# Reordering the first two batches of a fused sliding-window attention and hard-swish MLP: row-wise values in batch 0, weights asked for ahead of batch 2's second half

## The chip, the cores and the metric

The kernel runs on one core of a Trainium2 chip. The metric is the device time of one execution in microseconds (us). The core has five engines with an instruction queue each: TensorE (PE, with its weight loads shown as PEld), VectorE (DVE), ScalarE (ACT), GpSimd (POOL) and SyncE (SP). Each runs its own instructions in the order of the program and waits for the others by semaphores. DMAs are asked for by SP, ACT and POOL.

## The reference

Eight batches of eight heads with 576 positions of 64 channels go through causal attention in a window of 128 positions with a linear bias per head. The result is laid out as 4608 tokens of 512 channels and goes through an MLP with a hard-swish between its two matrices.

```python
rel = pos[:, None] - pos[None, :]
scores = where((rel >= 0) & (rel < 128), q @ k.T / 8 - slope[h] * abs(rel), -1e9)
attn = softmax(scores) @ v                     # 8 x 8 x 576 x 64
x = attn.transpose(0, 2, 1, 3).reshape(4608, 512)
h = x @ w_in                                   # 512 x 2048
out = (h * clip(h + 3, 0, 6) / 6) @ w_out      # 2048 x 512
```

## The kernel before

**Attention.** A group g is a pair of heads of one batch (`NP`, four, of them to a batch): batch b has the groups 4b to 4b+3, so batch 0 is groups 0 to 3, batch 1 groups 4 to 7, and group 8 opens batch 2. Since the window is 128, a block of 128 queries needs the scores with its own block of keys (the diagonal, `scores_diag`) and with the block ahead of it (the off-diagonal, `scores_off`). The bias comes either out of a table that a matmul adds into PSUM (`tables_diag`, `tables_off`, used for the diagonals of batch 0 and the off-diagonals of batches 0 and 1) or out of the exponential's bias on ACT, with a mask laid by POOL afterwards (`exp_diag`, `affine_select`). `attend` multiplies all five query blocks of a group with v and divides by the row sums on DVE; `back` transposes the result into `xT`, the MLP's input.

**Queries and keys.** For batch 0 each pair of heads is loaded by itself (`load_run`), cast to bf16 (`prepare`) and transposed by PE (`transposes`, 18 transposes of 64 by 64 for q and as many for k); each transpose bank is copied into `qTb` or `kTb`. Batches 1, 2 and part of 3 go by "doubles" of four heads: `load_double` (two requests of 288 KB), `prepare_double` (two casts on POOL), and `wide_double` or `double` (nine transposes, then one or two copies). `dp` is the half of the batch: dp 0 serves its first two groups, dp 1 its last two.

**MLP.** Tokens go in nine blocks of 512. For a block, 16 steps `moe_up` of four matmuls make the hidden layer (ACT takes a relu, DVE a scalar_tensor_tensor into `gbuf`), and 16 steps `moe_down` multiply with `w_out`. `fill(n)` issues the next n steps of that list, if the attention of their tokens is done (`done`). `up_begin` issues three of a step's four matmuls early. The order of everything else is written by hand: the scheduler keeps the program's order on each engine.

**Order at the start.** `first_batch` runs scores and exponentials of the four groups, then four times `attend` and `back`; two `up_begin` and the first fills stand between the last `back` and the double transposes of batch 1. `second_batch` runs groups 4 to 7 with fills between them, then `attend` and `back` of the four. `segment` does the rest, one group at a time: in the round of g it issues the scores and exponentials of g, the values of g - 1, and `stage_next(g)`, which holds the casts for what follows.

**Rooms and queues.** `ldbuf` 0 to 3 take the loads: q and k in 0 and 1, v of batches 0, 1 and 2 in 2, 3 and 2. Until w_out arrives, `w_out_sb` holds the probabilities of batch 0, and `gbuf[1]` those of batch 1. SP asks for q, v and k and for the stores; POOL asks for `w_in` (four chunks) and `w_out` (four chunks), in line with its casts and masks. The chunk of w_in numbered i is needed from step 4i of the first block on. A `memset` of one element into a room holds a later request back until that memset has run. PSUM banks: two of two banks each for scores ("sc"), one "av", two "h", one "o".

Of the kernel before, what the change touches and what calls it, by code (L numbers as in the profile page):

```python
# [10 lines left out]
FP32 = mybir.dt.float32  # L11
# [7 lines left out]
def kernel(  # L19
# [18 lines left out]
    LAST = S - 4 * 128  # L38
    SP = NQ * 128
    W = D + 1  # L40
    RP, RT = 64, 9
    slopes = [2.0 ** (-8.0 * (h + 1) / H) for h in range(H)]
    n_ms = d_ff // 128
    n_ks = d_model // 128
# [39 lines left out]
    ld = {}  # L84
    src_of = {"q": q, "k": k, "v": v}

    runs = {nm: ldbuf[i][:, 0:NP * RT * D].rearrange("p (g c) -> p g c", g=NP)
            for i, nm in enumerate("qk")}

    def load_run(g, nm, eng):  # L90
        b, hp = divmod(g, NP)
        eng.dma_start(out=runs[nm][:, hp, :],
                      in_=src_of[nm][b, 2 * hp:2 * hp + 2, :, :].rearrange(
                          "e (p t) d -> (e p) (t d)", t=RT))

    def load_double(b, dp, nm, eng):
        for e in range(2):
# [102 lines left out]
                                    in_=tbuf.rearrange("p h j c -> p (h j c)"))  # L200

    st = {}

    def prepare(g, copies):
        for nm, copy in zip("qk", copies):
            pr = prs.tile([128, RT * D], BF16, tag=f"pr{nm}", name="pr",
                          padded_shape=[128, 2 * RT * D])
            copy(out=pr, in_=runs[nm][:, g % NP, :])
            st[g, nm] = pr

    def transposes(g, copies):
        b, hp = divmod(g, NP)
        for nm, dst, copy in (("q", qTb[b % 2], copies[0]), ("k", kTb[b % 2], copies[1])):
            src = st.pop((g, nm))
            tp = ps_h.tile([128, RT, RP], BF16, tag="h", name="tp", padded_shape=[128, 16, 64])
            for t in range(RT):
                for e in range(2):
                    r = slice(e * D, (e + 1) * D)
                    nc.tensor.transpose(tp[r, t, :], src[r, ts(t, D)], ident[r, r])  # L219
            copy(out=dst[:, hp, :, :].rearrange("p j c -> p (j c)")[:, 0:S].rearrange(  # L220
                "p (a t) -> p a t", t=RT), in_=tp.rearrange("p t a -> p a t"))

    def prepare_double(b, dp, copies, nms="kq", early=None):
        for nm, copy in zip(nms, copies):
# [113 lines left out]
    def exp_full(g):  # L338
        for e in range(2):
            exp_diag(g, e)  # L340
        exp_off_full(g)
# [76 lines left out]
    def by_xbar(g):  # L418
        return g >= XB and g != XB + 2 and g != XB + 3
# [120 lines left out]
    def stage_next(g):  # L540
        b, hp = divmod(g, NP)
        nb = b + 1
        if g == 2 * NP:
            cast_tokens(2, "v")
        for n in LOADS.get(g, "").split():
            load_tokens(int(n[1]), n[0])
        if nb == 3 and hp < 2:
            prepare_double(3, hp, (P,), "k")
        if nb == 3 and hp == 1:
            cast_tokens(3, "q")  # L550
            xbar(3, "q")
        elif nb < B and nb > 3 and hp < 2:
            cast_tokens(nb, "qk"[hp])
            xbar(nb, "qk"[hp])
        if VCAST.get(g):
            cast_tokens(VCAST[g], "v")

    def first_batch():
# [6 lines left out]
        scores_diag(0)  # L565
        prepare(1, (P, V))
        transposes(1, (V, V))
        scores_off(0)
        exp_full(0)
        scores_diag(1)  # L570
        prepare(2, (P, P))
        tables_off(1)
        transposes(2, (V, V))
        scores_off(1)
        exp_full(1)
        scores_diag(2)
        prepare(3, (P, V))
        tables_off(2)
        transposes(3, (V, V))
        scores_off(2)  # L580
        exp_full(2)
        scores_diag(3)
        scores_off(3)
        exp_full(3)
        cast_v(0, 0, V)
# [12 lines left out]
        attend(2)  # L598
        back(1)
        prepare_double(1, 0, (P, P), early=second_w_in)  # L600
        attend(3)
        back(2)
        up_begin(0, 0, 3)
        back(3)
        wide_double(1, 0, "q", V)
        prepare_double(1, 1, (P, P))
        load_w_in(2)
        load_w_in(3)
        for dp in range(2):
            for nm in "kq":  # L610
                load_double(2, dp, nm, nc.sync)
        up_begin(0, 1, 3)
        done[0] = NP
        fill(1)
        wide_double(1, 0, "k", A)
        fill(2)

    def second_batch():
        for g in range(NP, 2 * NP - 1):
            if g < NP + 2:  # L620
                wide_double(1, 1, "kq"[g - NP], V)
            scores_diag(g)
            exp_diag(g, 0)
            exp_diag(g, 1)
            fill(1 if g == NP + 2 else 2)
            scores_off(g)
            exp_off_full(g)
            fill(2 if g == NP + 2 else 1)
            if g == NP + 1:
                cast_tokens(1, "v")  # L630
        for i in range(4):
            load_w_out(i)
        g = 2 * NP - 1
# [24 lines left out]
        wide_double(2, 0, "q", A)  # L658
        up_begin(1, 0, 3)
        back(2 * NP - 1)  # L660
        up_begin(1, 1, 3)
        done[0] = 2 * NP
        fill(2)
        scores_diag(2 * NP)
        scores_off(2 * NP)

    FILLS = {g: (1, 1, 1, 2, 0, 1, 1) for g in (9, 10, 11, 13, 14, 15)}

    def segment(lo, hi, fills):
        for g in range(lo, hi + 1):  # L670
            f = fills(g)
            if by_xbar(g - 2):
                done[0] = g - 1
            if lo < g < hi and g != 3 * NP + 1:
                scores(g)
            turn = {2 * NP: (2, 1, "k"), 2 * NP + 1: (2, 1, "q"),
                    2 * NP + 2: (3, 0, "k"), 2 * NP + 3: (3, 1, "k")}.get(g)
# [12 lines left out]
            if g > lo:  # L690
                values(g - 1, (0, 1, 2))
            fill(f[2])
            if g < hi:
                exp_off(g, 0)
            fill(f[3])
            if g < hi:
                exp_off(g, 1)
            if g > lo:
                values(g - 1, (3, 4))
            fill(f[4])  # L700
            if g > lo and by_xbar(g - 1):
# [14 lines left out]
    with tc.manual_schedule(engines=every):  # L716
        load_run(0, "k", nc.scalar)
        load_run(0, "q", nc.sync)
        load_run(1, "k", nc.scalar)
        load_run(1, "q", nc.sync)  # L720
        for g in (2, 3):
            load_run(g, "k", nc.scalar)
            load_run(g, "q", nc.sync)
        load_tokens(0, "v")
        constants()
        memsets()
        memsets_later()
# [36 lines left out]
```

## Time and profile before

| | |
|---|---|
| Median of three runs | 323.27 us (323.09 to 324.08) |
| The profiled execution | 323.3 us, its span 321.6 us, 1.7 us around it |
| PE busy | 312.4 us, 97% of the span |
| PEld, DVE, ACT, POOL busy | 167.6, 173.0, 195.6, 141.1 us |
| DMA | 51.90 MB moved, mean 161 GB/s |
| Granted clock of TensorE | 0.998 |

The span is that of the instructions in the trace. Busy time is the union of an engine's instructions; DMA requests and semaphores do not count. A matmul's shown duration has a tail that overlaps the next one: 512 columns are shown as some 0.38 us each while eight in a row take 1.73 us, 0.216 us from start to start.

### The profile page before, as it was taken

Reading aid. Unit: us, or ns where it says so; the run is one execution under the profiler, and the core shown is the slowest. Engines: PE = TensorE matmul, PEld = TensorE weight load, DVE = VectorE, ACT = ScalarE, POOL = GpSimd, SP = SyncE. Lnnn points to the kernel's source line nnn. Section 1 sums busy time; section 2 is a strip of 40 time slices with the busy share of each in tenths; the row PEclk is TensorE's granted clock in tenths of the full one; section 3 lists DMA queues with packets and bytes.
Section 4 is the critical chain, followed back from the end, with each engine's and each line's share of the span. In section 5 each row is a group of like instructions: output and inputs, shape, how many; then the busy total and the mean of one; then the engine's idle time right before and its main releaser. Section 6 shows DMA issues by size and latency. Waiting matters only on the chain.

```text
span 321.6 us, 7050 instructions
## 1 busy us (share of the span) xinstructions
PE 312.4 (97%) x2738; PEld 167.6 (52%) x2738; DVE 173.0 (54%) x338; ACT 195.6 (61%) x334; POOL 141.1 (44%) x249
## 2 busy tenths in 40 slices
PE   7889999999999999999999999999999999999996
PEld 5565465455555554554667654554554444444443
DVE  6667674554456555555555555555655455455510
ACT  3758976877767766766676667666764344244401
POOL 8455493594493767366745665463331000000000
PEclk9999999999999999999999999999999999999999
DMA  7999999899999999999999989922112200000112
GB/s 276 202 333 208 247 270 196 210 258 194 212 248 166 244 201 203 193 229 199 192 199 202 237 173 212 214 72 86 23 53 66 75 34 35 33 33 33 67 53 77
DMA packets 131425, 51.90 MB, mean 161 GB/s; under 512 B 118976, under 2 KB 123328, under 8 KB 131392
## 3 DMA queue, kind: packets, MB, share of 16 engines
q1 hardware_dynamic: 126160, 45.36, 66.2%
q0 software_dynamic: 4224, 4.19, 8.2%
q10 hardware_dynamic: 1008, 1.90, 1.6%
q8 instruction: 21, 0.34, 0.5%
q14 instruction: 12, 0.10, 0.1%
HBM read 36.70 MB, written 9.44 MB: 143 GB/s over the span
## 4 chain that ended last, share of the span: by engine, by line
PE 82%; DMA 10%; SPq 2%; POOL 2%; DVE 1%; ACT 1%; issue 1%; POOLq 0%
PE ops L501 37%; PE hps L451 33%; DMA w_out_sb<-in_moe_w_out_dram 5%; DMA ldbuf<-in_v_dram 3%; PE scd L296 3%; DMA ldbuf<-in_k_dram 2%; PE av L391 2%; SPq L112 2%; PE av L383 2%; PE sco L328 1%; PE ops L482 1%; PE w L153 1%; POOL w_out_sb L171 1%; PE tp L219 0%; ACT kTb L244 0%
## 5 line engine op out<-in xcount | busy, mean ns | idle before, releaser
L471 DVE SCALAR_TENSOR_TENSOR gbuf<-r,hps 128x512 bf16<-128x512 f32 x144 | 98.7, 687 | 102.5 <-ACT r L470 100.2
L470 ACT ACTIVATE r<-hps,bias 128x512 f32<-128x512 f32 x144 | 98.9, 689 | 88.9 <-PE hps L451 88.7
L451 PE MATMUL hps<-xT,w_in_sb 128*128 128x512 bf16 (+1 forms) x640 | 144.8, 358 | 0.5 <-ACT xT L438 0.3
L501 PE MATMUL ops<-w_out_sb,gbuf 128*128 128x512 bf16 x560 | 137.8, 379 | 0.3 <-DMA w_out_sb<-in_moe_w_out_dram 0.3
L451 PEld LDWEIGHTS <-w_in_sb 128*128 128x128 bf16 x640 | 59.2, 98 | 54.8 <-issue 0.8
L501 PEld LDWEIGHTS <-gbuf 128*128 128x128 bf16 x560 | 51.8, 98 | 56.7 <-issue 0.6
L354 POOL TENSOR_SCALAR_AFFINE_SELECT pd<-pd 128x512 bf16<-128x512 bf16 x48 | 29.7, 634 | 34.5 <-ACT pd L351 34.5
L364 POOL TENSOR_SCALAR_AFFINE_SELECT po<-po 128x512 bf16<-128x512 bf16 x48 | 30.3, 636 | 32.5 <-ACT po L361 32.3
L351 ACT ACTIVATE pd<-scd,bias_d 128x512 bf16<-128x512 f32 x48 | 31.7, 685 | 4.7 <-PE scd L296 4.7
L510 DVE COPY osb<-ops 128x512 f32<-128x512 f32 x33 | 22.7, 687 | 20.4 <-PE ops L501 20.2
L361 ACT ACTIVATE po<-sco,bias_o 128x512 bf16<-128x512 f32 x48 | 33.0, 688 | 0.0
L194 POOL CAST tbuf<-ldbuf 128x512 bf16<-128x512 f32 (+1 forms) x45 | 25.6, 614 | 16.7 <-DMA qTb<-tbuf 9.0
L402 DVE TENSOR_TENSOR avs<-av,rc 128x384 bf16<-128x384 f32 (+1 forms) x48 | 23.6, 491 | 1.6
L391 PEld LDWEIGHTS <-pd 128*128 128x128 bf16 x192 | 14.3, 97 | 8.3 <-issue 0.5
L383 PE MATMUL av<-vbuf,po 128*128 128x65 bf16 x192 | 18.0, 193 | 0.0
L391 PE MATMUL av<-vbuf,pd 128*128 128x65 bf16 x192 | 17.3, 194 | 0.3 <-ACT kTb L244 0.3
L187 POOL CAST vbuf<-ldbuf 128x1024 bf16<-128x1024 f32 x14 | 14.3, 1044 | 4.3 <-DMA ldbuf<-in_v_dram 4.3
L383 PEld LDWEIGHTS <-po 128*128 128x128 bf16 x192 | 14.3, 98 | 2.9 <-DVE avs L402 0.5
L367 ACT ACTIVATE p4buf<-sco,bias_d 128x64 bf16<-128x64 f32 x48 | 15.5, 324 | 0.0
L227 POOL CAST pr<-ldbuf 128x576 bf16<-128x576 f32 x20 | 12.9, 670 | 5.0 <-DMA ldbuf<-in_k_dram 3.1
L296 PE MATMUL scd<-qTb,kTb 64*128 64x128 bf16 x256 | 12.7, 219 | 1.7 <-DVE kTb L220 0.9
L296 PEld LDWEIGHTS <-kTb 64*128 64x128 bf16 x256 | 7.2, 94 | 13.4 <-issue 9.7
(96 smaller groups left out, 217.4 us busy)
## 6 DMA issues: line engine op xcount, KB each, us to landing
out_dram<-osb SPq DMA_DIRECT2D x33, 256.0 KB, 2.4
ldbuf<-in_v_dram SPq DMA_DIRECT2D x32, 256.0 KB, 5.6
ldbuf<-in_q_dram SPq DMA_DIRECT2D x20, 256.0 KB, 4.9
ldbuf<-in_k_dram SPq DMA_DIRECT2D x16, 256.0 KB, 4.5
ldbuf<-in_q_dram SPq DMA_DIRECT2D x12, 288.0 KB, 7.3
ldbuf<-in_k_dram SPq DMA_DIRECT2D x12, 288.0 KB, 7.6
w_in_sb<-in_moe_w_in_dram POOLq DMA_DIRECT2D x4, 512.0 KB, 8.8
w_out_sb<-in_moe_w_out_dram POOLq DMA_DIRECT2D x4, 512.0 KB, 11.6
```

The lines of the kernel that those rows point to most:

```text
L194: nc.gpsimd.tensor_copy(out=tbuf[:m, :, j, :], in_=s[:m, j, :, :].rearrange("p (i e) d -> p i (e d)", e=2))
L296: nc.tensor.matmul(scd[:, e, ts(j, 128)], lhsT=kT[r, j, :], rhs=qT[r, j, :], start=first, stop=first or j == 3)
L351: nc.scalar.activation(out=pd[:, e, :, :].rearrange("p j c -> p (j c)"), in_=sc[:, e, :], func=ACT.Exp, bias=bias_d[:, h:h + 1], scale=scale)
L354: nc.gpsimd.affine_select(out=pd[:, e, :, :], in_=pd[:, e, :, :], pattern=[[0, 4], [1, 128]], channel_multiplier=-1, base=0, compare_op=AL ...
L361: nc.scalar.activation(out=po[:, e, :, :].rearrange("p j c -> p (j c)"), in_=sc[:, e, :], func=ACT.Exp, bias=bias_o[:, h:h + 1], scale=scale)
L364: nc.gpsimd.affine_select(out=po[:, e, :, :], in_=po[:, e, :, :], pattern=[[0, 4], [-1, 128]], channel_multiplier=1, base=-1, compare_op=A ...
L383: nc.tensor.matmul(out_av, lhsT=po[:, e, qt % 4, :], rhs=vb[:, qt - 1, h, :], start=True, stop=False)
L391: nc.tensor.matmul(out_av, lhsT=d, rhs=vb[:, qt, h, :], start=(qt == 0), stop=True)
L451: nc.tensor.matmul(hps[:, lo:hi], lhsT=w_in_sb[:, ks, ts(ms, 128)], rhs=xT[:, ks, ds(src, hi - lo)], start=(ks == 0), stop=(ks == n_ks - 1))
L470: nc.scalar.activation(out=r6, in_=hps, func=ACT.Relu, bias=bias3[:, 0:1], scale=1.0 / 6.0)
L471: nc.vector.scalar_tensor_tensor(out=gts[nt][:, ms, :], in0=r6, scalar=1.0, in1=hps, op0=ALU.min, op1=ALU.mult)
L501: nc.tensor.matmul(ops[nt, sub], lhsT=gts[nt][:, ms, ts(sub, 128)], rhs=w_out_sb[:, ms, :], start=(ms == 0), stop=(ms == n_ms - 1))
```

## The change

In batch 0, a run of q or k is laid out as 96 partitions with six positions of both heads each, so that one transpose serves both heads: 6 for q and 6 for k where there were 18 each. The last run lies in `ldbuf[3]`. The order of transposes, score matmuls and exponentials is another, `memsets_later` moves from ahead of the first batch to behind batch 1's first transposes, and the values are worked out by rows of queries over several groups: `values_first` (blocks 0 to 2 of one group), `values_row` (one block of several groups), `values_last` (blocks 0 to 3 of group 3). Block 4, the last 64 positions, is worked out after `scores_diag(4)`. The two `up_begin` of block 0 are gone: the first MLP step stands behind `scores_diag(5)`.

In batch 1, the order of doubles, scores and fills is another, and `load_w_out` stands directly behind the casts of v. Of batch 2, the second double (dp 1) and v are asked for at the end of `second_batch`, behind a one-element memset on DVE; the casts of that double move from `second_batch` to `stage_next(8)`, its key transposes from the round of group 8 to that of group 9, and its query transposes to later in that same round.

```diff
     def prepare(g, copies):
...
-            pr = prs.tile([128, RT * D], BF16, tag=f"pr{nm}", name="pr",
-                          padded_shape=[128, 2 * RT * D])
-            copy(out=pr, in_=runs[nm][:, g % NP, :])
+            pr = prs.tile([RN, RK, 2, D], BF16, tag=f"pr{nm}", name="pr",
+                          padded_shape=[128, RT, 2, D])
+            copy(out=pr.rearrange("p t e d -> p e t d"),
+                 in_=runs[nm, g % NP].rearrange("p e (t d) -> p e t d", t=RK))
...
     def stage_next(g):
         if g == 2 * NP:
+            prepare_double(2, 1, (P, P))
+            for dp in range(2):
+                load_double(3, dp, "k", nc.sync)
+            load_tokens(3, "q")
             cast_tokens(2, "v")
...
     def first_batch():
...
+        scores_diag(3)
+        values_first(0, "av")
+        scores_off(3)
+        exp_full(3)
+        values_first(1, "h")
         cast_v(0, 3, V)
         cast_v(0, 4, P)
+        values_first(2, "h")
...
-        attend(0)
-        attend(1)
-        back(0)
-        attend(2)
-        back(1)
+        values_row((0, 1, 2), 3, "av")
+        values_last(3)
+        back_first(0, "o", (A,))
+        back_first(1, "h", (A,))
+        back_first(2, "h", (A,))
         prepare_double(1, 0, (P, P), early=second_w_in)
-        attend(3)
-        back(2)
-        up_begin(0, 0, 3)
-        back(3)
-        wide_double(1, 0, "q", V)
+        back_first(3, "o", (A, V))
+        wide_double(1, 0, "k", V)
+        wide_double(1, 0, "q", A)
+        memsets_later()
+        scores_diag(NP)
+        exp_diag(NP, 0)
+        exp_diag(NP, 1)
+        values_row((0, 1), 4, "av")
+        values_row((2, 3), 4, "h")
         prepare_double(1, 1, (P, P))
-        load_w_in(2)
-        load_w_in(3)
-        for dp in range(2):
-            for nm in "kq":
-                load_double(2, dp, nm, nc.sync)
-        up_begin(0, 1, 3)
+        for nm in "kq":
+            load_double(2, 0, nm, nc.sync)
+        scores_off(NP)
+        exp_off_full(NP)
+        back_row("o", A)
         done[0] = NP
-        fill(1)
-        wide_double(1, 0, "k", A)
-        fill(2)

     def second_batch():
...
+        scores_diag(NP + 1)
+        exp_diag(NP + 1, 0)
+        exp_diag(NP + 1, 1)
         load_w_in(2)
         load_w_in(3)
+        fill(2)
+        scores_off(NP + 1)
+        exp_off_full(NP + 1)
         fill(1)
+        wide_double(1, 1, "k", V)
+        fill(1)
+        wide_double(1, 1, "q", V)
+        fill(3)
+        cast_tokens(1, "v")
         for i in range(4):
             load_w_out(i)
+        g = NP + 2
...
         prepare_double(2, 0, (P, P))
-        nc.gpsimd.memset(ldbuf[2][:, 0:1], 0.0)
-        load_tokens(2, "v")
-        prepare_double(2, 1, (P, P))
-        for dp in range(2):
-            load_double(3, dp, "k", nc.sync)
-        load_tokens(3, "q")
...
+        nc.vector.memset(ldbuf[1][:, ds(2 * RT * D, 1)], 0.0)
         fill(2)
         scores_diag(2 * NP)
         scores_off(2 * NP)
+        for nm in "kq":
+            load_double(2, 1, nm, nc.sync)
+        load_tokens(2, "v")
```

More of the change, by code (lines that the diff above doesn't have):

```diff
@@ L40 @@
     W = D + 1
-    RP, RT = 64, 9
+    RT = 9
     slopes = [2.0 ** (-8.0 * (h + 1) / H) for h in range(H)]
@@ L85 @@
     src_of = {"q": q, "k": k, "v": v}
-    runs = {nm: ldbuf[i][:, 0:NP * RT * D].rearrange("p (g c) -> p g c", g=NP)
-            for i, nm in enumerate("qk")}
+    RN, RK = 96, 6
+    runs = {}
+    for i, nm in enumerate("qk"):
+        for hp in range(NP):
+            room, at0 = (ldbuf[i], hp * 2 * RK * D) if hp < 3 else (ldbuf[3], i * 2 * RK * D)
+            runs[nm, hp] = room[0:RN, ds(at0, 2 * RK * D)].rearrange("p (e c) -> p e c", e=2)
     def load_run(g, nm, eng):
         b, hp = divmod(g, NP)
-        eng.dma_start(out=runs[nm][:, hp, :],
+        eng.dma_start(out=runs[nm, hp],
                       in_=src_of[nm][b, 2 * hp:2 * hp + 2, :, :].rearrange(
-                          "e (p t) d -> (e p) (t d)", t=RT))
+                          "e (a t) d -> a e (t d)", t=RK))
     def load_double(b, dp, nm, eng):
@@ L213, in transposes @@
         for nm, dst, copy in (("q", qTb[b % 2], copies[0]), ("k", kTb[b % 2], copies[1])):
[L214 to L219, printed above, removed]
+            src = st.pop((g, nm)).rearrange("p t e d -> p t (e d)")
+            tp = ps_h.tile([128, RK, RN], BF16, tag="h", name="tp", padded_shape=[128, 8, 128])
+            for t in range(RK):
+                nc.tensor.transpose(tp[:, t, :], src[:, t, :], ident[0:RN, 0:RN])
             copy(out=dst[:, hp, :, :].rearrange("p j c -> p (j c)")[:, 0:S].rearrange(
-                "p (a t) -> p a t", t=RT), in_=tp.rearrange("p t a -> p a t"))
+                "p (a t) -> p a t", t=RK), in_=tp.rearrange("p t a -> p a t"))
     def prepare_double(b, dp, copies, nms="kq", early=None):
@@ L556, in stage_next, with values_first, normed @@
             cast_tokens(VCAST[g], "v")
+    def values_first(g, tag):
+        av = BANKS[tag].tile([128, 3, 2, W], FP32, tag=tag, name="av",
+                             padded_shape=[128, 3, 2, 85])
+        av_matmuls(g, range(3), lambda qt, e: av[:, qt, e, :])
+        normed(av, avs0[:, g, 0:3, :, :], 3)
+    def normed(av, to, n):
+        rc = small.tile([128, 4, 2, 1], FP32, tag="rcn", name="rcn")
+        nc.vector.reciprocal(rc[:, 0:n], av[:, :, :, D:W])
+        nc.vector.tensor_tensor(out=to, in0=av[:, :, :, 0:D],
+                                in1=rc[:, 0:n].to_broadcast([128, n, 2, D]), op=ALU.mult)
@@ new lines, in values_row @@
+    def values_row(gs, qt, tag):
+        n = len(gs)
+        if tag == "sc":
+            wide = ps_sc.tile([128, 2, 512], FP32, tag="sc", name="wide")
+            av = wide.rearrange("p s (g c) -> p (s g) c", c=256)[:, :, 0:2 * W].rearrange(
+                "p g (e c) -> p g e c", e=2)[:, 0:n]
+        else:
+            av = BANKS[tag].tile([128, n, 2, W], FP32, tag=tag, name="av",
+                                 padded_shape=[128, 3, 2, 85])
+        for i, g in enumerate(gs):
+            av_matmuls(g, (qt,), lambda _, e: av[:, i, e, :])
+        normed(av, avs0[:, gs[0]:gs[0] + n, qt, :, :], n)
@@ new lines, in values_last, with back_first @@
+    def values_last(g):
+        wide = ps_sc.tile([128, 2, 512], FP32, tag="sc", name="wide")
+        av = wide.rearrange("p s (g c) -> p (s g) c", c=256)[:, :, 0:2 * W].rearrange(
+            "p g (e c) -> p g e c", e=2)
+        av_matmuls(g, range(4), lambda qt, e: av[:, qt, e, :])
+        normed(av, avs0[:, g, 0:4, :, :], 4)
+    def back_first(g, tag, copies):
+        tp = BANKS[tag].tile([128, 512], BF16, tag=tag, name="tb", padded_shape=[128, 1024])
+        for j in range(4):
+            nc.tensor.transpose(tp[:, ts(j, 128)],
+                                avs0[:, g, j, :, :].rearrange("p e d -> p (e d)"), ident)
+        n = 512 // len(copies)
+        for i, copy in enumerate(copies):
+            copy(out=xT[:, g, ds(i * n, n)], in_=tp[:, ds(i * n, n)])
@@ L558, in first_batch, with back_row @@
+    def back_row(tag, copy):
+        tp = BANKS[tag].tile([128, NP, 128], BF16, tag=tag, name="tb",
+                             padded_shape=[128, 8, 128])
+        for g in range(NP):
+            nc.tensor.transpose(tp[:, g, :], avs0[:, g, 4, :, :].rearrange("p e d -> p (e d)"),
+                                ident)
+        copy(out=xT[:, :, ds(512, LAST)], in_=tp[:, :, 0:LAST])
     def first_batch():
@@ L565, in first_batch @@
         scores_diag(0)
+        scores_off(0)
+        exp_full(0)
         prepare(1, (P, V))
         transposes(1, (V, V))
-        scores_off(0)
-        exp_full(0)
         scores_diag(1)
         prepare(2, (P, P))
-        tables_off(1)
         transposes(2, (V, V))
@@ L575, in first_batch @@
         exp_full(1)
+        prepare(3, (P, P))
         scores_diag(2)
-        prepare(3, (P, V))
-        tables_off(2)
         transposes(3, (V, V))
@@ L581, in first_batch @@
         exp_full(2)
[L582 to L585, printed above, removed]
+        cast_v(0, 0, P)
         cast_v(0, 1, P)
@@ L675, in segment @@
                 scores(g)
-            turn = {2 * NP: (2, 1, "k"), 2 * NP + 1: (2, 1, "q"),
+            turn = {2 * NP + 1: (2, 1, "k"),
                     2 * NP + 2: (3, 0, "k"), 2 * NP + 3: (3, 1, "k")}.get(g)
@@ L699, in segment @@
                 values(g - 1, (3, 4))
+            if g == 2 * NP + 1:
+                double(2, 1, "q", 0, "av", A)
             fill(f[4])
+            if g == 2 * NP + 1:
+                double(2, 1, "q", 1, "h", V)
             if g > lo and by_xbar(g - 1):
```

26 lines of the change are left out of this document (11 added, 15 removed).

## The prediction

> **What bounds the kernel now.** I read the page first, then busy time by stretch, then PE's and POOL's timelines up to 70 us. The first two lines are busy time and the chain that ended last.
>
> ```profile
> PE 312.4 (97%) x2738; PEld 167.6 (52%) x2738; DVE 173.0 (54%) x338; ACT 195.6 (61%) x334; POOL 141.1 (44%) x249
> ...
> PE 82%; DMA 10%; SPq 2%; POOL 2%; DVE 1%; ACT 1%; issue 1%; POOLq 0%
> ```
>
> PE is busy 97% of the span and carries 82% of the chain. The next view, columns PE, PEld, DVE, ACT, POOL, clock, DMA share, GB/s, shows where it is not full.
>
> ```profile
> 7.00:19.00 12.00, 9.78 (x248) 6.45 (x240) 7.98 (x14) 8.72 (x9) 5.54 (x10) 1.00 1.11 234
> 19.00:25.00 6.00, 5.09 (x81) 3.93 (x78) 4.38 (x9) 2.34 (x5) 3.78 (x6) 1.00 1.10 352
> 25.00:42.00 17.00, 17.00 (x178) 9.01 (x176) 11.06 (x15) 16.76 (x26) 9.71 (x15) 1.00 1.13 244
> 42.00:62.00 20.00, 19.05 (x192) 10.64 (x190) 12.37 (x22) 14.73 (x26) 12.13 (x20) 1.00 1.09 205
> ```
>
> From 25 to 42 us PE never rests, with ACT close behind (16.76 of 17 us). After 42 us only about 1 us is missing up to 62. The holes lie ahead of 25 us, where scores, exponentials and copies of batch 0 alternate and busy time counts the tails of short matmuls. So the time is PE's work plus PE's waits. The change leaves that work as it is: 144 small transposes, 36 of which take 0.76 us, become 48 wider ones, which I put at 0.05 us (nine of 128 by 128 take 0.67 us with their tail), 0.6 us per group in either form. It is a question of waits alone. PE's timeline behind batch 0:
>
> ```profile
> 22.00 0.59 PE L451 MATMUL hps<-xT,w_in_sb 128*128 128x512 bf16 x2
> 22.89 0.38 PE L451 MATMUL hps<-xT,w_in_sb 128*128 128x512 bf16 x1 [0.29 <-ACT xT L438]
> ...
> 23.38 0.67 PE L254 MATMUL tp<-ident,pr 128*128 128x128 bf16 x9
> 23.88 1.03 PE L451 MATMUL hps<-xT,w_in_sb 128*128 128x512 bf16 x4
> 24.75 0.67 PE L254 MATMUL tp<-ident,pr 128*128 128x128 bf16 x9
> 25.25 1.24 PE L451 MATMUL hps<-xT,w_in_sb 128*128 128x512 bf16 x5
> 26.33 0.67 PE L254 MATMUL tp<-ident,pr 128*128 128x128 bf16 x9
> 26.93 0.40 PE L296 MATMUL scd<-qTb,kTb 64*128 64x128 bf16 x8
> ...
> 59.05 1.02 PE L501 MATMUL ops<-w_out_sb,gbuf 128*128 128x512 bf16 x4 [0.33 <-DMA w_out_sb<-in_moe_w_out_dram]
> ```
>
> While batch 1's q and k arrive, PE is fed with 12 up matmuls (2, 1, 4 and 5) and the third double; `scores_diag(4)` follows at 26.93. POOL's timeline gives the arrivals and requests that matter:
>
> ```profile
> 20.93 2.17 POOL L227 CAST pr<-ldbuf 128x576 bf16<-128x576 f32 x3 [1.49 <-DMA ldbuf<-in_k_dram]
> ...
> 27.22 0.67 POOL L227 CAST pr<-ldbuf 128x576 bf16<-128x576 f32 x1 [0.73 <-DMA ldbuf<-in_q_dram]
> 27.83 1.48 POOL L166 DMA_DIRECT2D w_in_sb<-in_moe_w_in_dram  x2
> ...
> 47.86 2.49 POOL L227 CAST pr<-ldbuf 128x576 bf16<-128x576 f32 x4
> ...
> 60.68 0.29 POOL L370 TENSOR_SCALAR_AFFINE_SELECT p4buf<-p4buf 128x128 bf16<-128x128 bf16 x1
> ...
> 62.56 1.05 POOL L187 CAST vbuf<-ldbuf 128x1024 bf16<-128x1024 f32 x1 [0.60 <-DMA ldbuf<-in_v_dram]
> ```
>
> The row at 20.93 is three casts for dp 0, the last begun on q's arrival at about 22.4 and done at 23.1. The w_in request at 27.83 holds chunks 2 and 3. The four casts at 47.86 are those of batch 2's second double, in an empty stretch; 60.68 is group 8's last mask, and batch 2's v casts follow.
>
> **Part 1, batch 0: no gain on the path.** Runs of 288 KB in 96 partitions move the same bytes; a cast there is 768 elements per partition for 576, estimated 0.67 x 4/3 = 0.89 us on POOL. With no memsets ahead of it, POOL begins q of group 1 at its landing, 6.1 instead of 6.53. I lay the order out by row times (copy 0.76, exponential of 1024 columns 1.02, transposes 0.6): diagonal exponentials begin at 8.4, 11.1, 13.5 and 15.7 (before 8.38, 10.69, 13.56, 16.41), the last exponential ends at 17.9 (18.36). Values, divisions (0.2 + 0.56 us) and `back_first` end on PE at 21.2, where the last `back` ended at 23.5. This gain of 2.3 us hides behind an arrival: batch 1's q is cast at 23.1 as before, since SP asks for the same loads in the same order and the w_in chunk 0 request moves only from 12.4 to about 12.7.
>
> **Part 2, the front: +2.0 us.** PE has no MLP step to put there now. Double k at 21.9, double q at 23.1 to 23.6, its copy on ACT 1.11 us, `scores_diag(4)` at 25.0. Then two `values_row` (0.5), `scores_off(4)` (0.85 with tables), `back_row`, `scores_diag(5)`, and the first step at 27.3. By 27.25 the kernel before had done 12 up matmuls (12 x 0.216 = 2.6 us) and a third double (0.5); the changed one has `scores_off(4)` and `scores_diag(5)` ahead (0.85 + 0.24). It is 2.6 + 0.5 - 1.1 = 2.0 us of PE work behind. Bounds: 1.4, if ACT and DVE hand over without delay; 3.0, if the copies queue (the key copy sits behind `back_first(3)`'s DVE half, which waits for ACT's half).
>
> **Part 3, to the values of batch 1: +0.2 and +1.0.** Double copies of 1.35 us on DVE stand between the hidden-layer steps; laid out, step 6 waits for a bank, `scores_diag(6)` for the query copy, step 7 for a bank, 0.7 us in all, against some 0.5 us of small waits before. The w_in request for chunks 2 and 3 now stands on POOL behind 2.7 us of memsets, the masks of group 4 (waiting for exponentials that end at 26.6), four casts (2.5) and the masks of group 5: about 30.9 for 27.83. Queued behind it are the v casts and w_out. A chunk takes 6.3 to 9.5 us from request to landing (median 8.8), so it lands at 37.2 to 40.4; step 8 wants it at 37.2. The wait is 0 to 3.2 us; I take 1.0, nearest to chunk 2's own 6.3 us, as v of batch 1 was ahead of it there and here is nearly through. The Trainium skill ("DMA: Bandwidth & Descriptors", Queues, rings and completion order) has each DMA engine go round the queues packet by packet, so POOL's chunk would share with SP's loads rather than stand behind them; by it the wait would be nearer 0.5 us and the sum 0.5 us less. The trace agrees in kind: a v load asked for at 27.98 landed after 10.47 us, while the two chunks requested from 27.83 passed it.
>
> **Part 4, w_out and batch 2: -0.5 and +1.2.** w_out is asked for at about 35 for 41.2; its four chunks, 3.2 to 3.4 us between landings in the trace, follow w_in's last and are through by 57, so the 0.33 us wait at 59.05 goes, and a bank wait beside the moved double, 0.2. The doubles (2, 1) are asked for at about 53, when DVE reaches its memset (which waits for casts long done and delays no hidden-layer step behind it), and v behind them on SP; 1.2 + 1.2 MB arrive by 62 to 65 at the 200 GB/s of those slices. They are late for nothing by themselves. But their four casts (2.49 us) leave an empty stretch for the place between 60.68 and 60.92: group 8's last mask, then four casts, then v. Two v casts (2 x 1.0) end 4.5 us after the mask; before, values of group 8 began 3.6 us after it (64.53), of which 0.3 was the w_out wait. PE waits 1.2 us, part of it already in front of double (2, 1, k). Bounds 0.3 (casts end before PE comes) and 1.8. Masks of group 9 come 2.7 us later on POOL, 71.5 for 69; their values want them after 75. The other moved requests (k and q of batch 3) stand behind one store on SP, and their casts have over 2 us of room.
>
> **Sum.** Against the profiled 323.3 us (span 321.6 and 1.7 around it), which is the median to 0.03: 2.0 + 0.2 + 1.0 - 0.5 + 1.2 = +3.9, so 327.2 us. All lows: 1.4 + 0 + 0 - 0.7 + 0.3 = +1.0, 324.3; all highs: 3.0 + 0.5 + 3.2 - 0.3 + 1.8 = +8.2, 331.5; both together are unlikely, 324.3 to 329.5 is this case's own range.
>
> **Rivals.**
> *ACT was the bound (faster).* If ACT and not PE sets the stretch from 25 to 42 us, the change gives it group 4's exponentials at 25.3 instead of 27.68 and one copy of 1.11 us less, for 0.3 more: its 17.1 us of work up to group 7's last exponential would end at 25.3 + 16.3 = 41.6, for 42.1. With 0.5 of part 4 and the casts in time, 323.3 - 0.5 - 0.5 = 322.3, or 321.9 if batch 1's back chain gains too. For it: 16.76 of 17 us. Against: PE is 17.00 of 17 and has none of ACT's waits there. It decides if PE does its steps with ACT never idle over 0.3 us between 25 and 42. Chance 0.10.
> *Most of it is covered.* q and k of batch 1 land earlier (at best 0.9 us, then DVE's key copy holds `scores_diag(4)` at 24.05), w_in arrives in time, the casts cost 0.3: 2.0 - 0.9 + 0.2 - 0.5 + 0.3 = +1.1 or somewhat less, 324.0. For: the first requests go out unhindered. Against: the DMA share is over 1.0 there. Chance 0.12.
> *The clock falls.* In this trace the first matmuls ran at half pace (512 columns in 0.43 us until about 6.4 us, from 1.43), and later ones at 0.216. From 19.3 to 25.0 the changed PE has only 2.0 us of work, all transposes. If that returns it to half pace for as long as at the start, 5 us, 2.5 us of work takes twice its time: 327.2 + 2.5 = 329.7. Before, the stretch from 19 to 25 us (5.09 of 6 busy) showed no slow matmul. Chance 0.10. The Trainium skill ("TensorE: Matmul & The Clock Gate", Part 1) states that an idle window of about 3.4 us halves the clock and that as long a busy one restores it; by it the cost would be an estimated 1.7 us.
> *v of batch 2 comes late.* The change would not do what it says if w_out, asked for sooner, were not through by 57 and held the double and v behind it: v's fourth piece landing after 67 adds what is over, up to 2 us: 329. Chance 0.08.
>
> **How the numbers follow.** About 0.3%, 1 us, is what a measurement of this kernel can tell from no change. Forecast 0.60 (327.2), clock 0.10, late v 0.08, covered 0.12 (of it 0.05 slower by over 0.3%, 0.07 within), ACT 0.10 (of it 0.09 faster by over 0.3%, 0.01 within). Slower 0.83, same 0.08, faster 0.09. The range leaves out the ACT case below and the highest ends above: 323.4 to 330.0.
>
> **What would show it.** `scores_diag(4)` near 25 and the first up matmul near 27.3, PE's busy time in 19 to 25 us under 4 us; the w_in request near 31 and a wait for w_in before step 8; no wait for w_out; the casts of the double (2, 1) on POOL just behind group 8's masks and PE waiting for POOL near 66 to 68; the rest of the chain shifted as a whole. I am wrong if the first up matmul stands before 25 us, or if PE's waits behind 27 us add up to less than before.

## The result and the profile after

The changed kernel takes 333.4 us (median of 4 runs, 332.55 to 334.4) where the kernel before takes 323.4 beside it. The ratio is 1.031, with a 95% interval of 1.027 to 1.034. It is slower, as forecast, but by 10.0 us and not by 3.9, and lies above the range. The profiled execution took 333.56 us, with a span of 331.8. Executions over 1.5% longer than the fastest of the same kernel count as disturbed and are left out of the ratios, as 342.03 us of the kernel with w_in early, whose trace is therefore not read, and 335.79 us of the kernel with batch 2 as before.

The first view is the page: busy time, and the granted clock in 40 slices (one slice is 8.3 us).

```profile
PE 314.0 (95%) x2642; PEld 168.0 (51%) x2642; DVE 172.7 (52%) x343; ACT 196.0 (59%) x335; POOL 141.1 (43%) x250
...
PEclk9995999999999999999999999999999999999999
```

PE's busy time grew by only 1.6 us (314.0 for 312.4), and its share fell from 97 to 95%. The new thing is the 5 in the clock row: in the fourth slice, 25 to 33 us, TensorE ran at half pace. By stretch (columns as in the prediction: PE, PEld, DVE, ACT, POOL, clock, DMA share, GB/s):

```profile
19.00:25.00 6.00, 3.07 (x64) 2.52 (x60) 3.51 (x10) 2.58 (x5) 2.91 (x7) 0.99 1.09 345
25.00:32.00 7.00, 5.40 (x64) 3.74 (x62) 2.48 (x5) 3.29 (x4) 5.08 (x13) 0.52 1.19 263
32.00:42.00 10.00, 9.45 (x72) 4.79 (x72) 6.75 (x9) 7.52 (x14) 9.29 (x13) 1.00 0.96 216
42.00:62.00 20.00, 17.93 (x212) 10.54 (x213) 11.71 (x22) 14.85 (x23) 4.88 (x8) 1.00 0.86 150
```

From 19 to 25 us PE is busy for 3.07 of 6 us (before 5.09). Then 5.40 of 7 us are busy, but at 0.52 of the clock, at which the same work takes longer. PE's and POOL's timelines show what it waits for:

```profile
22.60 0.38 PE L602 MATMUL tb<-ident,gbuf 128*128 128x128 bf16 x4 [0.23 <-ACT xT L606]
24.50 0.81 PE L259 MATMUL tp<-ident,pr 128*128 128x128 bf16 x9 [1.51 <-POOL pr L232]
25.70 1.14 PE L259 MATMUL tp<-ident,pr 128*128 128x128 bf16 x9 [0.40 <-POOL pr L232]
28.05 0.61 PE L301 MATMUL scd<-qTb,kTb 64*128 64x128 bf16 x8 [1.21 <-ACT qTb L261]
...
31.93 1.90 PE L456 MATMUL hps<-xT,w_in_sb 128*128 128x512 bf16 x8
...
43.54 0.82 PE L456 MATMUL hps<-xT,w_in_sb 128*128 128x512 bf16 x3 [1.73 <-DMA w_in_sb<-in_moe_w_in_dram]
```

```profile
29.52 1.22 POOL L359 TENSOR_SCALAR_AFFINE_SELECT gbuf<-gbuf 128x512 bf16<-128x512 bf16 x2 [1.86 <-ACT gbuf L356]
30.70 2.48 POOL L232 CAST pr<-ldbuf 128x576 bf16<-128x576 f32 x4
33.14 1.21 POOL L359 TENSOR_SCALAR_AFFINE_SELECT gbuf<-gbuf 128x512 bf16<-128x512 bf16 x2
34.31 1.51 POOL L170 DMA_DIRECT2D w_in_sb<-in_moe_w_in_dram  x2
```

`scores_diag(4)` stands at 28.05 (forecast 25.0) and the first step at 31.93 (27.3). The nine transposes at 25.70 take 1.14 us where nine took 0.67 before. The request for w_in chunks 2 and 3 comes at 34.31 (forecast 30.9), lands at 43.49, and PE waits 1.73 us for it at step 8. In the kernel before that step began at 34.37. Further on, PE's waits from 66 to 80 us (total, times, longest):

```profile
PE tp L247 <- DVE avs L407: 1.0, 1, 1.0
PE av L396 <- POOL vbuf L191: 0.6, 1, 0.6
PE tp L247 <- POOL pr L232: 0.4, 1, 0.4
```

In order of time these are, from the last line up, the wait for the casts of the double (2, 1), the one for v's casts behind them, and the one at the later query double. The kernel before has a single wait of 0.2 us from 62 to 80 us. The wait for w_out is gone.

One thing the forecast did not expect stands at the very start. The eight runs of batch 0 land from 5.18 to 12.57 us, before from 4.51 to 9.46, though they are the same bytes asked for at the same times.

### The profile page after: what moved, and what is told of

Same layout as the page of the kernel before. It is cut to its first block, busy times and chain, and to the rows that moved or that the text cites. A ratio compares the mean times of both kernels' runs of the same rounds, so it can differ in the third digit from the quotient of the medians.

```text
span 331.8 us, 6865 instructions
## 1 busy us (share of the span) xinstructions
PE 314.0 (95%) x2642; PEld 168.0 (51%) x2642; DVE 172.7 (52%) x343; ACT 196.0 (59%) x335; POOL 141.1 (43%) x250
## 4 chain that ended last, share of the span: by engine, by line
PE 81%; DMA 9%; ACT 3%; POOL 3%; DVE 2%; issue 1%; ACTq 0%; POOLq 0%
PE ops L506 36%; PE hps L456 34%; DMA ldbuf<-in_k_dram 4%; DMA ldbuf<-in_v_dram 3%; DMA w_in_sb<-in_moe_w_in_dram 3%; PE scd L301 2%; PE av L396 2%; POOL pr L232 2%; PE av L388 2%; PE sco L333 1%; PE ops L487 1%; ACT r L475 1%; ACT kTb L249 1%; POOL gbuf L359 1%; PE tp L247 1%
```

## The experiments

**The theory from these views:** four costs. The 96-partition runs arrive late; the hole ahead of `scores_diag(4)` halves the clock; w_in is asked for too late; batch 2's moved double costs more than 1.2 us. The rival is that the new order of batches 0 and 1 itself is the cost, and the waits merely show where it comes out. First, single parts on either kernel. The kernel before was run beside every group of experiments; its medians there are 323.7, 323.7 and 324.0 us (323.4 beside the changed kernel), so half a microsecond between runs of different groups says nothing.

### The layout alone, on the kernel before

```diff
+    RN, RK = 96, 6
...
-            for t in range(RT):
-                for e in range(2):
-                    r = slice(e * D, (e + 1) * D)
-                    nc.tensor.transpose(tp[r, t, :], src[r, ts(t, D)], ident[r, r])
+            for t in range(RK):
+                nc.tensor.transpose(tp[:, t, :], src[:, t, :], ident[0:RN, 0:RN])
```

> The kernel before with one part of the change alone: the runs of batch 0's q and k in 96 partitions with 1536-byte pieces (loads, casts, 6 + 6 transposes); order and all else as before. Late-loads theory: the last run lands near 12.6 us as in the changed kernel (9.5 before), v of batch 0 and the doubles of batch 1 follow some 2 to 3 us later, and the time is 325.3 to 326.4 us. Rival, my prediction's own assumption that the layout is free: landings within 0.3 us of before, 323.3 us.

It took 325.95 us, ratio 1.008 (1.005 to 1.010): 2.3 us, where the forecast had put nothing. The last run lands at 12.28 us and batch 1's first q at 24.41, as in the changed kernel. The clock of the profiled execution stays at 1.00. PE does not lose the time at the runs themselves: the last pair's `scores_diag` begins at 15.91 us, before at 15.98. It loses it at what stands behind them in the queue. The five loads of batch 0's v land from 13.24 to 18.85 us (before 10.63 to 16.03), and PE waits for their casts, which it did not do before:

```profile
PE wide L394 <- DVE vbuf L185: 0.9, 1, 0.9
PE wide L394 <- POOL vbuf L185: 0.4, 1, 0.4
```

The part brings other casts and transposes with it, so that the loads are the whole of the 2.3 us is not shown apart from them.

### The changed kernel with the old layout

```diff
-    RT = 9
+    RP, RT = 64, 9
...
-    RN, RK = 96, 6
```

> The changed kernel with that one part undone: runs in 128 partitions with 2304-byte pieces and 18 + 18 transposes per group; the changed order stays. Late-loads theory: q of batch 1 is cast near 23 us for 25.6, the front moves up by 2 us or more, 329.4 to 331.4 us. If the layout is free: 333 us. The clock theory adds: if PE's idle stretch shrinks enough, the granted clock stays at 1.00 between 25 and 32 us and another 2 us go; if the row still shows about half, they stay.

It took 331.62 us, ratio 1.024 (1.021 to 1.028), 1.8 us less than the changed kernel. PE's timeline:

```profile
24.80 0.40 PE L298 MATMUL scd<-qTb,kTb 64*128 64x128 bf16 x8 [1.21 <-ACT qTb L258]
...
27.38 1.90 PE L453 MATMUL hps<-xT,w_in_sb 128*128 128x512 bf16 x8
...
40.20 1.89 PE L453 MATMUL hps<-xT,w_in_sb 128*128 128x512 bf16 x4 [2.93 <-DMA w_in_sb<-in_moe_w_in_dram]
...
43.34 2.76 PE L453 MATMUL hps<-xT,w_in_sb 128*128 128x512 bf16 x12
```

This is the kernel that the prediction had described: `scores_diag(4)` at 24.80 (25.0), the first step at 27.38 (27.3), the w_in request at 30.85 (30.9), step 8 wanted at 37.27 (37.2). The chunk lands at 40.16, at the far end of the forecast's 37.2 to 40.4. The wait is 2.93 us, and behind it the clock is at half: four matmuls of 512 columns in 1.89 us for 1.02, until 43.2 us. From 19 to 25 us PE is busy for 3.41 of 6 us (3.07 in the changed kernel), and from 25 to 32 us, where the changed kernel had its half pace, this one has none:

```profile
25.00:32.00 7.00, 6.94 (x88) 3.98 (x83) 2.62 (x7) 6.41 (x10) 5.94 (x10) 1.00 1.13 220
```

### Three up steps back in the hole

```diff
         back_first(3, "o", (A, V))
+        done[0] = NP
+        fill(1)
         wide_double(1, 0, "k", V)
+        fill(1)
         wide_double(1, 0, "q", A)
+        fill(1)
...
         load_w_in(3)
-        fill(2)
         scores_off(NP + 1)
         exp_off_full(NP + 1)
-        fill(1)
```

> The changed kernel with three up steps put back into the gap: one behind the last back_first, one behind each of the two double transposes (the fills behind scores_diag(5) lose as many). Theory of order and clock: PE has 2.6 us of matmuls while q of batch 1 arrives, the granted clock stays at 1.00, and both the 2.0 us of work behind and some 2.3 us of half clock go: 329.0 to 330.0 us. If only the order counts and the clock falls all the same: 331.4. If the front is late for its loads alone: 333.

It took 335.51 us, ratio 1.038 (1.035 to 1.041): 2.1 us slower than the changed kernel, against the expectation. The hole was filled as meant: the clock is 1.00 from 19 to 32 us, and by then 12 up matmuls have begun, where the changed kernel had begun one. But w_in chunk 2 lands at 43.55 (43.49 in the changed kernel), and the step that needs it cannot move:

```profile
43.60 1.89 PE L456 MATMUL hps<-xT,w_in_sb 128*128 128x512 bf16 x4 [5.04 <-DMA w_in_sb<-in_moe_w_in_dram]
```

What was gained ahead became a wait of 5.04 us, and the clock fell in that wait instead: half pace until 47.7 us, 0.86 in the mean from 42 to 62 us. From 43.60 to 47.73 us that is 4.1 us of work at half pace, an estimated 2.1 us of time, as much as this kernel is slower. So the late request was a floor under everything ahead of step 8: what is gained or lost ahead of it does not show, and half pace behind it does. In the changed kernel the hole hid the floor.

### Part 4 alone, on the kernel before

Batch 2's second double and v are late, and w_out stands behind batch 1's v, as in the changed kernel.

```diff
         exp_diag(g, 1)
         prepare_double(2, 0, (P, P))
-        nc.gpsimd.memset(ldbuf[2][:, 0:1], 0.0)
-        load_tokens(2, "v")
-        prepare_double(2, 1, (P, P))
...
         if g == 2 * NP:
+            prepare_double(2, 1, (P, P))
```

> The kernel before with the last part of the change alone: w_out asked for directly behind the casts of batch 1's v, batch 2's second double and v asked for at the end of batch 1, the casts of that double in stage_next(8), its transposes in the round of group 9. Theory of the casts: the wait for w_out goes (-0.3 to -0.5), PE waits for POOL's casts near 66 us and for the later double (+1.2 to +2.6): 324.0 to 325.5 us. Rival: the casts are hidden, 322.8 to 323.3.

It took 325.73 us, ratio 1.008 (1.005 to 1.011): 2.0 us. PE's waits from 62 to 80 us are the same 1.0, 0.6 and 0.4 us as in the changed kernel. The profiled execution was the longest of the six (327.82 us); it waits besides for 2.19 us for w_in at 37.30, which the profiled execution of the kernel before does not.

### w_in asked for early

```diff
+        load_w_in(2)
+        load_w_in(3)
         memsets_later()
         scores_diag(NP)
...
-        load_w_in(2)
-        load_w_in(3)
         fill(2)
```

> The changed kernel with nothing else altered than that w_in chunks 2 and 3 are asked for directly behind the first double transposes of batch 1, ahead of POOL's memsets and group 4's masks. Theory (the late request behind the chain of casts, masks and memsets sets step 8 at 43.5 us): request near 25.7 instead of 34.3, landing before 36, PE's wait for w_in (1.7 us) gone, so 333.4 - 1.7 = 331.5 to 332.0 (masks and casts of POOL move by two requests, 1.5 us, which is hidden). The hole and the half clock between 24 and 32 us stay (25 to 32 us near 0.5). Rival (what is gained at step 8 is lost again to a later cast or bank wait, the early steps being bound by DVE and ACT): 333.0 to 334.

Its median is 331.87 us, ratio 1.024 (1.021 to 1.027): 1.5 us less, within the theory's range. Where the chunk lands is not shown, for want of a trace to read; that the half pace stays shows in a mean clock of 0.984 to 0.990.

### w_in early and the three steps

Both edits together:

```diff
+        fill(1)
         wide_double(1, 0, "q", A)
+        fill(1)
+        load_w_in(2)
+        load_w_in(3)
         memsets_later()
```

> The changed kernel with three up steps in the gap before scores_diag(4) and with w_in chunks 2 and 3 asked for early. Three steps alone made it 335.5 since PE then stood 5 us at step 8. Theory (the hole in the front, with its half clock, and the late w_in are two costs of which the second covered the first): both go together, clock 1.00 to 62 us, no wait for w_in over 0.5 us: 333.4 less 1.7 (w_in), 2.3 (clock) and about 1.5 to 2.0 (the hole filled) = 327.4 to 328.0. Rival (the early steps' order of banks and copies is the cost, w_in hides it): not below 330.

It took 329.09 us, ratio 1.016 (1.012 to 1.019). In the profiled execution the clock is 1.00 throughout and the wait for w_in is 0.6 us. The same three steps that cost 2.1 us alone now gain 2.8. This is 1.1 us above the theory's end and 0.9 below the rival's 330: that the order has a cost of its own may hold for a part.

### Filling the hole with matmuls of no use

```diff
         back_first(3, "o", (A, V))
+        warm_up(20)
         wide_double(1, 0, "k", V)
+        warm_up(20)
         wide_double(1, 0, "q", A)
+        warm_up(20)
```

w_in is early here too. The 60 matmuls go into a PSUM tile that nobody reads.

> The changed kernel with w_in chunks 2 and 3 asked for early (331.9 alone) and with 60 matmuls of 128 by 128 without use laid into PE's waits between the last back_first and scores_diag(4), 20 ahead of each double and 20 ahead of scores_diag(4). They do no work of the kernel; 20 take 1.1 us at full pace and each of the three waits is 1.5 to 1.9 us. Theory (the idle PE loses its clock, and the half pace costs 2 us that are not hidden once w_in is there): clock 1.00 from 19 to 42 us and 329.5 to 330.2. Rival (half pace costs nothing, since PE waits for casts and copies of POOL, DVE and ACT in that stretch anyway): 331.5 to 332.5, with the clock at 1.00 or not.

It took 330.39 us, ratio 1.020 (1.017 to 1.023): 1.5 us less than without them, though PE does more, and 0.2 above the theory's end. The mean clock is 0.995 to 1.000. The stretch that stood at 0.52:

```profile
25.00:32.00 7.00, 6.70 (x100) 4.70 (x100) 1.82 (x6) 5.46 (x9) 6.87 (x15) 1.00 1.18 239
```

So of the 2.8 us that the steps gained, about 1.5 are put down to the clock, and the 1.3 that are left to the work that they bring forward. With 1.4 and 1.8 us between the executions of these two kernels, the split is a rough one.

### Batch 2 as before, all else as changed

```diff
         prepare_double(2, 0, (P, P))
+        nc.gpsimd.memset(ldbuf[2][:, 0:1], 0.0)
+        load_tokens(2, "v")
+        prepare_double(2, 1, (P, P))
```

> The changed kernel with batch 2's second double and v asked for, cast and transposed where the kernel before does it; w_out stays behind batch 1's v casts. Theory (the part of batch 2 costs the 2.0 to 2.3 us that it cost alone on the kernel before, independently of the front): 331.2, with PE's waits for casts and values at 70 to 77 us (1.0, 0.6 and 0.4 us) gone. Rival (the late front already leaves that cost hidden): 333 or more.

Inconclusive: 329.48, 332.64, 333.48 and 335.79 us; the ratio, from the first three, is 1.024 (1.017 to 1.032). In the profiled execution (329.48) the waits at 70 to 77 us are gone, the half pace from 25 to 32 us is there, and w_in was asked for at 32.90 and landed at 41.52. The other three were not profiled. What moves this kernel by 6 us from run to run stays open.

### All four undone

The old layout, the three steps, w_in early, batch 2 as before; the row-wise values, the order of batch 1 and w_out behind v stay.

```diff
+    RP, RT = 64, 9
...
+        fill(1)
+        load_w_in(2)
+        load_w_in(3)
         memsets_later()
...
         prepare_double(2, 0, (P, P))
+        nc.gpsimd.memset(ldbuf[2][:, 0:1], 0.0)
+        load_tokens(2, "v")
+        prepare_double(2, 1, (P, P))
```

> The changed kernel with all four suspected costs undone: 128-partition runs, three up steps in the gap, w_in chunks 2 and 3 asked for early, batch 2 as before; what stays is batch 0's row-wise order of values, the order of batch 1 and w_out behind v's casts. Theory (these four are the whole loss and add up: 1.8 to 2.3 for the layout, 1.7 + 2.3 + 1.8 for w_in, clock and hole, 2.0 for batch 2): 323.0 to 324.5, equal to the kernel before. Rival (the orders of batch 0 and 1 cost something of their own): 326 or more; a result under 322.5 would say that the row-wise order is a gain once w_in is there.

It took 324.91 us, ratio 1.003 (1.001 to 1.005), 1.2 us above the kernel before. From `after_ups_win` that is 4.2 us, close to the 4.3 of the layout's 2.3 and batch 2's 2.0, each measured alone on the kernel before. The four costs are the loss but for 1.2 us and add up, once w_in no longer hides one behind another. What is left, 1.2 us, falls by remainder to the orders:

```profile
25.00:32.00 7.00, 4.83 (x78) 3.26 (x77) 2.94 (x8) 5.84 (x9) 6.34 (x13) 1.00 1.21 204
```

PE is busy there for 4.83 of 7 us, where the kernel before is busy for all 7. No run takes the orders apart.

### Why the 96 partitions load late

The pieces shrank from 2304 to 1536 bytes, and the partitions from 128 to 96. Two layouts on the kernel before tell these apart: 64 partitions of two pieces of 2304 bytes (the last pair's run lies in `gbuf[0]` there), and 128 partitions of two pieces of 1152.

The first line is that of `before_64`, the others are those of `before_1152`.

```diff
+    RN, RK = 64, 9
...
-                          "e (p t) d -> (e p) (t d)", t=RT))
+                          "e (p t) d -> (e p) (t d)", t=RT).rearrange("p (s c) -> p s c", s=2))
```

> The kernel before with batch 0's runs in 64 partitions of two pieces of 2304 bytes each (nine transposes for a run, both heads at once), other orders as before. It tells what made the loads of the 96-partition layout late. Theory (the pieces of 1536 bytes take as long, some 100 ns, as those of 2304, so the same bytes need 1.5 times the packets' time): loads as in the kernel before, last run landed near 9.5 us, 390 GB/s in 5 to 8 us, and about 323.7, up to 1 us more for casts of 1152 elements in fewer partitions. Rival (fewer partitions are loaded more slowly, whatever the piece): 64 partitions are later than 96, last run after 12.6 us, 326.5 or more.

> The kernel before with batch 0's runs in 128 partitions as before, but each partition's 2304 bytes as two pieces of 1152 (a gap behind each in the room). Theory (time per piece): 16 engines of 1152 bytes in about 95 to 100 ns are 185 to 195 GB/s, the 2.36 MB of runs need 12 us and not 6, the last run lands near 15 us for 9.5, and the time is 326.5 to 329. Rival (the number of partitions decides): loads and time as before, 323.7.

The rival of both expectations was right, but for landings 1.1 us later in `before_1152`. `before_64` took 328.86 us, ratio 1.015 (1.013 to 1.018); `before_1152` took 324.15, ratio 1.0005 (0.9985 to 1.0025). The stretch from 4 to 8 us, with the rate as the last number, in the kernel before, `before_96`, `before_64` and `before_1152`:

```profile
4.00:8.00 4.00, 3.26 (x54) 2.35 (x54) 2.24 (x7) 1.83 (x4) 3.42 (x8) 1.00 1.05 404
```

```profile
4.00:8.00 4.00, 3.00 (x38) 1.92 (x37) 2.26 (x7) 2.07 (x5) 3.30 (x7) 1.00 1.09 258
```

```profile
4.00:8.00 4.00, 3.25 (x34) 2.27 (x32) 2.31 (x6) 2.61 (x4) 2.92 (x7) 1.00 1.05 207
```

```profile
4.00:8.00 4.00, 2.72 (x60) 1.86 (x58) 2.21 (x7) 2.65 (x5) 2.57 (x7) 1.00 1.05 338
```

The DMA share (the number ahead of the rate) is full in all four. Half the partitions give half the rate with the very same piece; half the piece in all partitions gives 338 GB/s of 404. In the trace's packets from 5 to 8 us, 2304 bytes take 93 ns (median) to 128 partitions and 185 to 64; 1152 bytes take 51 ns, and 1536 bytes to 96 partitions 100. The last run lands at 9.46, 12.28, 15.19 and 10.54 us. In `before_64` the clock falls too, to 0.50 from 9.7 to 19.9 us, so its 4.9 us are not the loads' alone.

The Trainium skill ("SBUF — State Buffer", Door 1) has a rule that fits: a load's rate goes by how many of 16 ports its partitions reach, and partitions 0 to 63 reach only eight. The trace agrees for 64 partitions (207 of 404 GB/s). For 96, by that map two thirds of the bytes share eight ports, an estimated three quarters of the full rate, 303 GB/s; the trace shows 258, so the rule gives the direction and not all of the size. That the ports are the cause is the page's; the runs show the partitions.

### w_out alone

```diff
             if g == NP + 1:
                 cast_tokens(1, "v")
-        for i in range(4):
-            load_w_out(i)
+                for i in range(4):
+                    load_w_out(i)
```

> The kernel before with one thing moved: w_out asked for directly behind the casts of batch 1's v, as in the changed kernel. Theory (w_out is 0.33 us late at 59 us in the kernel before): the wait goes, 323.3 to 323.5 for 323.7. Rival (an earlier w_out takes DMA time from batch 2's doubles or is late for another reason, or holds masks and casts on POOL by its four requests of 0.75 us): 323.7 to 325.

It took 323.70 us beside 324.01, ratio 0.999 (0.998 to 1.001): no difference that can be measured. The wait for w_out is gone from its trace, and the 0.33 us that it was would lie within the interval. No version that was run beats the kernel before by a difference that can be measured.

## Why the prediction was wrong in size

The direction and most of the mechanism were right; two terms of the sum were mis-sized, one was put at nothing, and one effect given as a rival happened on top. Even all highs together, 331.5 us, do not reach 333.4.

- **Part 1, "no gain on the path", and "runs of 288 KB in 96 partitions move the same bytes".** This is the step that failed first: a term put at nothing on the bytes alone. They move the same bytes at 258 GB/s for 404. Alone it costs 2.3 us. It pushes batch 0's v, the first w_in request (15.36 for the forecast's 12.7) and batch 1's loads behind it (q landed at 24.45 for 22.38), and with them the front: with the old layout both ends of Part 2, 24.80 and 27.38, are within 0.2 us of the forecast.
- **Part 2, the front, +2.0.** The mechanism was right and its times too, layout aside. Filling the hole gained 2.8 us once w_in was early, of which about 1.5 is the clock, no part of this term, and about 1.3 the missing work (bounds were 1.4 to 3.0). The 1.2 us that remain in `after_undone` may belong here and to the small waits of Part 3; no run shows it.
- **Part 3, w_in chunk 2, +1.0.** The request was right without the layout (30.85 for 30.9). The choice within the bounds was wrong: I took a wait of 1.0 us from chunk 2's own 6.3 us; it took 9.3, and the wait was 2.9 of at most 3.2. The median of the four chunks in the trace, 8.8 us, was the better row. The 6.3 was also a lucky one: in the five other traces in which chunk 2 is asked for in the old order it took 7.0 to 8.2 us. By the rule on queues cited there the wait would have been near 0.5; the runs go against that. What the trace was said to show for it was thin: of the two chunks one was asked for ahead of that v load, and the other landed 0.5 us ahead of it. In the changed kernel itself the wait is only 1.7, since the late front covers the rest, and 1.5 us came back when it was removed.
- **Rival, the clock falls (0.10).** It happened: 0.52 from 25 to 32 us. But with the front as forecast (`after_128`) the profiled execution does not have it there; it took the late loads as well, which widened the hole. In `after_128` it came with the wait for w_in. So a term for the clock belonged in the sum, at the longest wait. Its cost, estimated at 2.5 us, came out at about 1.5.
- **Part 4, -0.5 and +1.2.** The casts behind group 8's masks are there as drawn, but the part cost 2.0 us and not 0.7. The forecast counted one wait ahead of v's casts (0.3 to 1.8); the trace shows 0.4 for the double's casts, 0.6 for v's, and 1.0 at the second, moved query double, which it had not costed. Of the 0.5 for w_out nothing can be measured: the wait is gone, and `before_wout` is the same within its interval.
- **The other rivals.** That ACT was the bound falls: it is busy for 10.8 of 17 us from 25 to 42 (3.29 and 7.52). That most is covered falls: q of batch 1 and w_in both came later and not earlier. That v of batch 2 is late falls too: w_out was through by 56.45, v landed from 68.07 to 72.30 us, and POOL cast it straight behind the double's four casts (68.86 to 73.32 us without a wait), so that the 0.6 us are POOL's order.

For the old-layout kernel the forecast can be put right from its own terms: 327.2, plus 1.9 for the wait (2.93 for 1.0), plus 1.3 for Part 4, plus an estimated 1.5 for the 3.0 us at half pace behind the wait, is 331.9; it measured 331.62. This is a sum made with the result known, and no test: of its four executions the one with the lowest mean clock, 0.988 for 0.995, was the fastest (330.61 us). The way back from the changed kernel, in us:

| step | time | what it returned |
|---|---|---|
| as changed | 333.4 | |
| w_in early | 331.9 | 1.5 |
| and three steps in the hole | 329.1 | 2.8 (clock about 1.5) |
| and old layout, batch 2 as before | 324.9 | 4.2 (alone 2.3 and 2.0) |
| the kernel before | 323.7 | 1.2, by remainder the orders |

## What to carry to other kernels

Ask of a new layout not only how many bytes it moves but into how many partitions: at the head of a kernel, where everything waits for the first loads, a layout that landed 2.8 us later cost 2.3 us of time. When work is taken out of a stretch, add the clock to its price, and look for the next thing that becomes due: a weight asked for in line with casts and masks is a floor, and work brought forward ahead of it turns into a wait. Where a cost lies between bounds, take the middle of the rows, or of more traces, and not the one that fits best.

## What the runs showed of the hardware

A wait of 2.93 us sufficed to bring TensorE to half pace, and 3.0 us of work ended it (`after_128`); a wait of 2.19 us left the clock at 1.00 (`before_b2late`). In the changed kernel the clock fell at about 24.9 us with no wait over 1.51 us; 22.97 to 24.50 was idle, and PE had had holes since 19 us. The Trainium skill ("TensorE: Matmul & The Clock Gate", Part 1) speaks of an idle window of about 3.4 us; the way back agrees in `after_128`, and the fall came after shorter waits than that.

Half pace came in steps of one length: by the granted clock it lasted 3.42 us in `after_128` (39.78 to 43.20), 6.83 in the changed kernel (24.89 to 31.72) and in `after_ups` (40.90 to 47.73), and 10.24 in `before_64` (9.66 to 19.90), that is once, twice and three times some 3.41 us. In the 3.41 us ahead of these falls PE was not idle throughout but busy for 0.90, 1.45, 1.07 and 1.72 us; in the 3.42 us before that, the changed kernel was busy for 2.44 us and kept its clock. How little work brings the fall was not measured.

The rate of a load went by its partitions: 404 GB/s into 128, 258 into 96 and 207 into 64 (4 to 8 us).
